# Attention and mixture of experts in one kernel: logits once per chunk, the first output product and half of the key work later, and p v in two halves

## The chip, the cores and the metric

The kernel runs on one core of a Trainium2 chip. The metric is the device time of one execution in microseconds, the median of several runs. TensorE (PE in the profile) does the matrix products into PSUM, VectorE (DVE) and ScalarE (ACT) move results from PSUM to SBUF and do the arithmetic between, GpSimd (POOL) works in SBUF, and SyncE (SP) issues most of the transfers.

## The reference

Four batches of 12288 queries of width 128 attend to 768 keys each, which are averages of 4 x 4 pixels through one weight matrix; keys and values are the same array. The attention's output is the input of a mixture of 8 experts, of which each token uses one.

```python
kv_pool = kv.reshape(B, H // r, r, W // r, r, C).mean(axis=(2, 4))
k = v = kv_pool.reshape(B, -1, C) @ w_sr
s = (q @ k.transpose(0, 2, 1)) / sqrt(C)
a = exp(s - s.max(-1)); a /= a.sum(-1) + 1e-09
x = a @ v                                   # 49152 tokens of 128
logits = x @ w_gate
e_idx = argmax(logits); gate_w = softmax(logits)[e_idx]
eom = 1 / (1 + exp(-(x @ w_output_gate)))
for e in range(E):                          # 8 experts
    h = maximum(x[mask] @ w1[e], 0)         # 128 -> 1024
    out[mask] = gate_w * eom[:, e] * (h @ w2[e])
```

## The kernel before

**Groups, chunks, rounds.** The tokens are worked in 96 groups of 512 (GT), 24 per batch; four groups are a chunk of 2048, for which the experts are chosen together (the last chunk is split into units of three groups and one). The main loop runs over rounds i, each of eight slots s. In round i the scores of group i are computed (slots 0, 2, 4 and 6, 128 tokens each), the product p v of group i-1, and the expert's two layers of an earlier group, with the expert that most tokens of the batch are taken to want, chosen from the mean of the keys. The tokens whose own choice is another expert are written to lists by GpSimd, 16 indirect transfers a chunk (L688), and worked at the end.

**Precision.** Each product of full precision is made of three products of half precision: a value is split into a high half (ScalarE, a copy with rounding) and a low half (VectorE, the difference), and high x high, high x low and low x high are added in PSUM. So a group's p v is 18 matmuls of 512 columns (6 key blocks x 3; L523), a product h of the first expert layer is 3 (L773 to L775), a product y of the second layer is 3 (L788 to L790), and 128 tokens' scores are 6 of 384 columns (L466 to L470).

**Order by hand.** The schedule is manual: every engine works in the order in which the loop issues. Within a slot the letters of `ORD = "shxryfue"` say what follows: s the scores (`qk`), h one product of the first layer (`moe_h`), x the exponential (`qk_exp`, ScalarE L487), r its rounding to two halves (ScalarE L500, GpSimd L501), y one product of the second layer (`moe_y`), u p v (`pv`, slot 5), e the events that were put off to this slot. The products y with f = 5, 6 and 7 come at the start of a slot, the others at y, where four h are ahead of them (`yb == hb - 4`). One slot in 30 leaves h and y out, so that they drift back against the scores.

**PSUM.** psA has two buffers of two banks for the scores. psH has three banks in turn under the tag "H": for every h, for U (the result of p v), for the logits `lg`, and for their transposes `lT`. psY has a single bank for Y, in which the eight products y of a group add up; ScalarE copies it to `ys` (L793) after f = 7, and the next group's f = 0 writes the bank anew. A product h is evicted by ScalarE (HH, L778) and then by VectorE (HL, L779); U by ScalarE (L527) and VectorE (L528) to U2.

**Logits.** `logits(i)` is called for each group, in slot 1 of round i+2. It multiplies U2's two halves by the gate weights, 32 columns wide (wgA and wgB), as 8 matmuls of 128 columns in four column strips of the array (L540, L543), and ScalarE copies the 128 columns of the result (L546). After a chunk's last group the four results are transposed (`logits_turn`, L564) and `routing` runs over the next slots, in steps on VectorE.

**Keys of the next batch.** `kv_prep` is a generator that does a step a slot: it pools the pixels on GpSimd, transposes and multiplies on TensorE (L301, L236), scales, and splits the keys to K2 (L342 on ScalarE, L343 on VectorE, in two halves of 384). V2 is a transposing transfer of K2. Then the mean of the keys times the gate weights chooses the expert (`choice`, L247, put as a hook into the scores of slot 0 or 2), `w_load` fetches its weights and `w_split` splits them (L754 to L761).

Of the kernel before, what the change touches and what calls it, by code (L numbers as in the profile page):

```python
# [20 lines left out]
F32 = mybir.dt.float32  # L21
# [4 lines left out]
AF = mybir.ActivationFunctionType  # L26
ALU = mybir.AluOpType
# [3 lines left out]
ts = bass.ts  # L31

P = 128
C = 128
E = 8
FF = 1024
NFB = FF // P
NK = 768
NKB = NK // P
GT = 512  # L40
GB = GT // P
# [5 lines left out]
PSH = 11  # L47
EPS = 1e-9
BIG = float(1 << 22)
LAG = 2  # L50
OL = 7
US2 = 2.0 ** -28


class Cfg:
# [27 lines left out]
    QL, QT, QN = 0, 3, 6  # L83
# [4 lines left out]
    QK = 2  # L88
    UT, UO = 3, 7
    UD, UDS = 0, 0  # L90
    UB = 9
    MT, MO = 4, 2
    KV0, KVP, KVD = (2, 1), (23, 23), 8
    PHD = (0, 2)
# [3 lines left out]
def body(ctx, tc, q, kv, w_sr, w_gate, w_og, w1, w2, out, cfg=Cfg):  # L98
    nc = tc.nc
    pe, act, dve, pool, sp = nc.tensor, nc.scalar, nc.vector, nc.gpsimd, nc.sync  # L100
    NB, NCH = cfg.NB, cfg.NC
    NG = NB * NCH * CG
# [3 lines left out]
    UN = [(c * CG, CG) for c in range(NCK - 1)]  # L106
# [3 lines left out]
    unit = {g0 + g: (u, g) for u, (g0, n) in enumerate(UN) for g in range(n)}  # L110
# [4 lines left out]
    rt = ctx.enter_context(tc.tile_pool(name="rt", bufs=1))  # L115
    psA = ctx.enter_context(tc.tile_pool(name="psA", bufs=2, space=PSUM))
    psH = ctx.enter_context(tc.tile_pool(name="psH", bufs=3, space=PSUM))
# [58 lines left out]
    wgA = cst.tile([P, 4 * E], F16, name="wgA")  # L176
    wgB = cst.tile([P, 4 * E], F16, name="wgB")
    g3 = cst.tile([P, 4], F32, name="g3")
# [13 lines left out]
    qscale = float(C) ** -0.5  # L192
# [35 lines left out]
    def kv_prep(b, fast):  # L228
# [17 lines left out]
        def choice(ap):  # L246
            pe.matmul(ap, sb, wg[:, 0:E], start=True, stop=True)  # L247
            got.append(ap)
# [22 lines left out]
        for k in range(NKB):  # L271
            while KVN[b][0] < 4 * (k + 1) or not fast and now[0] < KVI[(b, k)] + cfg.KVD:
                yield
            if fast:
                if k + 1 < NKB:
                    kv_add(b, k + 1)
                x, y = kvst.pop((b, k))
                ps = psA.tile([P, 2, 512], F32, tag="A", name=f"kvt{b}_{k}")
# [11 lines left out]
            x, y = kvst.pop((b, k))  # L290
# [9 lines left out]
            ps = psA.tile([P, 2, 512], F32, tag="A", name=f"kvt{b}_{k}")  # L300
# [8 lines left out]
        e2 = kvp.tile([P, 7], F32, tag="ve2", name=f"ve2{b}")  # L309
# [16 lines left out]
        ps = psA.tile([P, 2, 512], F32, tag="A", name=f"vmp{b}")  # L326
# [10 lines left out]
            chosen()  # L337
        K2 = kvp.tile([P, 2, NK], F16, tag="K2", name=f"K2{b}")
        V2 = kvp.tile([P, 2 * NKB, C], F16, tag="V2", name=f"V2{b}")
        for h in range(2):  # L340
            hh = ts(h, NK // 2)
            act.activation(K2[:, 0, hh], kT[:, hh], AF.Copy, scale=e2[:, 2:3])  # L342
            dve.scalar_tensor_tensor(K2[:, 1, hh], kT[:, hh], e2[:, 2:3], K2[:, 0, hh], op0=ALU.mult, op1=ALU.subtract)  # L343
            if not h:
                dve.tensor_scalar(e2[:, 3:4], e2[:, 0:1], 2.0 ** -14 * qscale, None, op0=ALU.mult)
                dve.tensor_scalar(e2[:, 4:5], e2[:, 2:3], US2, None, op0=ALU.mult)
                dve.tensor_scalar(e2[:, 5:6], e2[:, 4:5], EPS * 2.0 ** PSH, None, op0=ALU.mult)
        if fast:
            next(QP[0], None)
        KVT[b] = (K2, V2, e2[:, 3:4], e2[:, 4:6])  # L350
# [5 lines left out]
        if not fast:  # L356
            yield
            mean()
            hooks.append((now[0] + 1, lambda S: choice(S[:, 0, 384:384 + E])))
            while not got:  # L360
                yield
            yield
# [13 lines left out]
    KVT, CHO, CHI, WL, QP = {}, {}, {}, [], []  # L376


    QT, QM, QS, PTt, US, UF, UT, SUMS, LP, LG = {}, {}, {}, {}, {}, {}, {}, {}, {}, {}

    def tokens(ap3, i):

# [61 lines left out]
    hooks, now, mid = [], [0], [False]  # L444
# [73 lines left out]
    def pv(i, lo, hi, cols=slice(0, GT)):  # L518
        ops = pv_ops(i)
        if i not in PVP:  # L520
            PVP[i] = psH.tile([P, GT], F32, tag="H", name=f"U{i}")
        for n in range(lo, hi):
            pe.matmul(PVP[i][:, cols], ops[n][0], ops[n][1][:, cols], start=(n == 0), stop=(n == len(ops) - 1))  # L523
        if hi == len(ops) and cols.stop == GT:
            u = PVP.pop(i)
            U2 = wk.tile([P, 2, GT], F16, tag="U2", bufs=cfg.UB, name=f"U2{i}")
            act.activation(U2[:, 0, :], u, AF.Copy, scale=US2)  # L527
            dve.scalar_tensor_tensor(U2[:, 1, :], u, US2, U2[:, 0, :], op0=ALU.mult, op1=ALU.subtract)  # L528
            US[i] = (U2[:, 0, :], U2[:, 1, :])
            UF[i] = U2  # L530
            del PTt[i]

    def logits(i):

        UH, UL = US[i]
        c, g = unit[i]
        ps = psH.tile([P, GT], F32, tag="H", name=f"lg{i}")
        for j in range(GB):
            r = slice(32 * j, 32 * j + 32)
            pe.matmul(ps[r, 0:P], wgA, UH[:, ts(j, P)], start=True, stop=False, tile_position=(0, 32 * j))  # L540
        for j in range(GB):
            r = slice(32 * j, 32 * j + 32)
            pe.matmul(ps[r, 0:P], wgB, UL[:, ts(j, P)], start=False, stop=True, tile_position=(0, 32 * j))  # L543
        if g == 0:
            LP[c] = rt.tile([P, GT], F32, tag="lgp", bufs=1, name=f"lgp{c}")
        act.activation(LP[c][:, ts(g, P)], ps[:, 0:P], AF.Copy, scale=g3[:, 2:3])  # L546

    def u_turn(i):

# [232 lines left out]
    def moe_y(i, f):  # L782
        w2h, w2l = WT[i // GPB][2:4]
        HH, HL = HS.pop((i, f))
        if f == 0:
            YP[i] = psY.tile([P, GT], F32, tag="Y", name=f"Y{i}")
        Y = YP[i]
        pe.matmul(Y, w2h[:, ts(f, P)], HH, start=(f == 0), stop=False)  # L788
        pe.matmul(Y, w2l[:, ts(f, P)], HH, start=False, stop=False)  # L789
        pe.matmul(Y, w2h[:, ts(f, P)], HL, start=False, stop=(f == NFB - 1))  # L790
        if f == NFB - 1:
            ys = wk.tile([P, GT], F32, tag="ys", bufs=OL, name=f"ys{i}")
            act.activation(ys, YP.pop(i), AF.Copy)  # L793
            OST[i] = ys
            del US[i]
# [173 lines left out]
    with tc.manual_schedule(engines={pool.engine, sp.engine, pe.engine, act.engine, dve.engine}):  # L969
# [26 lines left out]
        hb = yb = 0  # L996
# [8 lines left out]
        def at(n, f, *args):  # L1005
            events.setdefault(8 * i + s + n, []).append((f, *args))

        def after_values(ri, rc):
            logits(ri)
            if rc is not None:  # L1010
                def turn():
                    logits_turn(rc)
                    rts.append([routing(rc), 0, rc])
                at(cfg.RG, turn)
            n = max(0, 8 * cfg.UD + cfg.UDS * ri - now[0])
            at(cfg.UT + n, u_turn, ri)
            at(cfg.UO + n, u_out, ri)
# [34 lines left out]
        for i in range(NG + OL):  # L1052
            att = i < NG
            pvi, ri, mi, oi = i - 1, i - 2, i - LAG, i - OL - 1
            if att and i % GPB == k0(i) and i // GPB + 1 < NB:
                kl, kp = kv_load(i // GPB + 1), kv_prep(i // GPB + 1, False)
            rc = unit[ri][0] if 0 <= ri < NG and ri + 1 == sum(UN[unit[ri][0]]) else None
            for s in range(8):
# [4 lines left out]
                if s == 0 and i in (NG - 1, NG):  # L1063
                    at(7, after_values, i - 1, unit[i - 1][0] if sum(UN[unit[i - 1][0]]) == i else None)
                go = mi >= 0 and not (att and (8 * i + s) % cfg.SK == cfg.SO)
                if go and yb % 8 >= 5 and yb < 8 * NG:
                    moe_y(*divmod(yb, 8))
                    yb += 1
                for o in cfg.ORD if mi >= 0 else cfg.ORDA:
                    if o == "h" and go:  # L1070
                        if hb < 8 * NG:
                            moe_h(*divmod(hb, 8))
                            hb += 1
                    if o == "s" and att and s % 2 == 0:
                        qk(i, s // 2)
                        while late:
                            qk_round(*late.pop(0))
                    if o == "x" and att and s % 2 == 0:
                        qk_exp(i, s // 2)
                    if o == "r" and att and s % 2:  # L1080
                        if s // 2 in cfg.PHD and i < LAG:
                            late.append((i, s // 2))
                        else:
                            qk_round(i, s // 2)
                    if o == "f" and s == cfg.PVS:
                        mid[0] = True
                        if ws:
                            next(ws, None)
                        mid[0] = False
                        if att and i % CG != 3:  # L1090
                            routes(1)
                    if o == "u":
                        for d, h in cfg.PVA:
                            x = i - d // 8
                            if d % 8 == s and 0 <= x < LAG - 1:
                                pv(x, 0, 3 * NKB, slice(h * GT // 2, (h + 1) * GT // 2))
                        if LAG - 1 <= pvi < NG and s == cfg.PVS:
                            pv(pvi, 0, 3 * NKB)
                    if o == "y" and go and yb == hb - 4:
                        moe_y(*divmod(yb, 8))  # L1100
                        yb += 1
                    if o == "e":
                        for f, *args in events.pop(8 * i + s, ()):
                            f(*args)
# [10 lines left out]
                if att and s in (cfg.QLA[i] if i < len(cfg.QLA) else (cfg.QL,)):  # L1115
# [5 lines left out]
                    while qa < qn:  # L1121
                        c = qa // CG
# [5 lines left out]
                if att and s == cfg.QL:  # L1128
                    n = min(ql + 2, i + cfg.QN + 1, NG)
# [7 lines left out]
                if kp:  # L1137
                    n = (8 * (i % GPB - k0(i)) + s) % cfg.KVP[min(i // GPB, 1)]
# [25 lines left out]
        while events:  # L1164
            i, s = divmod(min(events), 8)
# [39 lines left out]
```

## Time and profile before

| | |
|---|---|
| median of 3 runs | 1961.77 us (1961.56 to 1962.83) |
| the profiled execution | 1980.32 us, span 1978.6 us |
| TensorE busy | 1888.6 us, 95% of the span |
| VectorE, ScalarE, GpSimd busy | 1503.3, 1330.9, 1158.6 us |
| mean granted TensorE clock | 0.991 |
| queue of SyncE's transfers | 309.18 MB, 77.9% of 16 engines' time |

A matmul's record spans its whole passage through the array, so that consecutive ones overlap: a 512-column matmul lasts 0.38 us in the records, but the next one starts 0.215 us after it. The pace is read from the starts. "Idle before" is the time that an engine stood still in front of an instruction, and the arrow names what ended the wait.

### The profile page before, as it was taken

What the parts mean: (1) busy time and instruction counts of PE and PEld (TensorE: products, weight loads), DVE (VectorE), ACT (ScalarE), POOL (GpSimd) and SP (SyncE); (2) the same over time, 40 slices, a digit from 0 to 9 for tenths busy, and PEclk for the clock granted to TensorE, in tenths of its full rate; (3) what the DMA queues carried; (4) which work ended last, traced back from release to release, by engine and by line L of the source; (5) the groups of instructions that cost most, each with busy time, mean ns of one, the idle gap of its engine ahead of it and who ended that gap; (6) DMA issues with size and microseconds to landing.
All of it is one profiled execution on the core that took longest, in us unless ns stands there. A gap on an engine that the chain in (4) does not pass through costs nothing. (4 is left out here: it accounts for less than half of the span.)

```text
span 1978.6 us, 31039 instructions
## 1 busy us (share of the span) xinstructions
PE 1888.6 (95%) x10225; PEld 948.2 (48%) x10225; DVE 1503.3 (76%) x3005; ACT 1330.9 (67%) x2462; POOL 1158.6 (59%) x996
## 2 busy tenths in 40 slices
PE   6999999999999999999999999999999999999967
PEld 4444455444444544444444444444444444445434
DVE  6776777878878778778788787787787877886753
ACT  3767677667677776667776776666767767677623
POOL 3437567656576676663765756645556556456551
PEclk9999999999999999999999999999999999999999
DMA  7888888887888888787978888869688787877622
GB/s 234 156 164 162 171 160 179 159 163 154 165 174 166 182 165 160 158 167 153 166 167 167 171 170 177 159 135 181 135 159 159 140 166 156 143 158 140 130 63 67
DMA packets 884018, 311.64 MB, mean 158 GB/s; under 512 B 827584, under 2 KB 833857, under 8 KB 883856
## 3 DMA queue, kind: packets, MB, share of 16 engines
q1 hardware_dynamic: 870944, 309.18, 77.9%
q0 software_dynamic: 12480, 0.40, 0.5%
q8 instruction: 81, 1.33, 0.3%
q14 instruction: 81, 0.66, 0.1%
q10 hardware_dynamic: 432, 0.07, 0.0%
HBM read 56.83 MB, written 51.25 MB: 55 GB/s over the span
## 5 line engine op out<-in xcount | busy, mean ns | idle before, releaser
L501 POOL TENSOR_TENSOR ph<-pr,ph 128x768 f16<-128x768 f32 x384 | 632.3, 1647 | 651.4 <-ACT ph L500 383.6
L779 DVE SCALAR_TENSOR_TENSOR HL<-H,HH 128x512 f16<-128x512 f32 x768 | 526.9, 686 | 164.5 <-ACT HH L778 124.4
L778 ACT ACTIVATE HH<-H 128x512 f16<-128x512 f32 x768 | 455.1, 593 | 237.6 <-PE H L775 192.9
L487 ACT ACTIVATE pr<-S,nm,qm 128x768 f32<-128x768 f32 x384 | 380.5, 991 | 175.5 <-DVE nm L473 140.0
L688 POOL DMA_INDIRECT scr<-rw,idx x384 | 382.7, 997 | 95.0 <-issue 86.0
L472 DVE TENSOR_REDUCE nm<-S 128x1 f32<-128x768 f32 x384 | 365.0, 951 | 43.3 <-PE S L470 35.2
L523 PE MATMUL U<-PT,V 128*128 128x512 f16 (+1 forms) x1746 | 392.4, 379 | 5.8 <-DVE HL L779 3.4
L500 ACT ACTIVATE ph<-pr 128x768 f16<-128x768 f32 x380 | 319.7, 841 | 2.4 <-DMA PT<-ph 1.7
L773 PE MATMUL H<-U,w 128*128 128x512 f16 x768 | 292.0, 380 | 14.2 <-DVE HL L779 11.8
L788 PE MATMUL Y<-HH,w 128*128 128x512 f16 x768 | 291.7, 380 | 9.4 <-ACT ys L793 8.0
L790 PE MATMUL Y<-HL,w 128*128 128x512 f16 x768 | 291.3, 379 | 1.2 <-issue 1.0
L774 PE MATMUL H<-U,w 128*128 128x512 f16 x768 | 292.0, 380 | 0.0
L775 PE MATMUL H<-U,w 128*128 128x512 f16 x768 | 291.9, 380 | 0.0
L789 PE MATMUL Y<-HH,w 128*128 128x512 f16 x768 | 291.3, 379 | 0.2 <-issue 0.2
L523 PEld LDWEIGHTS <-V 128*128 128x128 f16 x1746 | 172.0, 99 | 211.3 <-issue 9.9
L466 PE MATMUL S<-K,qT 128*128 128x384 f16 x768 | 188.9, 328 | 15.3 <-ACT pr L487 6.4
L470 PE MATMUL S<-K,qT 128*128 128x384 f16 x768 | 188.5, 327 | 1.3 <-DVE qT L442 1.3
L468 PE MATMUL S<-K,qT 128*128 128x384 f16 x768 | 188.4, 327 | 0.5 <-DVE K L343 0.5
L527 ACT ACTIVATE U<-U 128x512 f16<-128x512 f32 x96 | 57.2, 596 | 136.1 <-PE U L523 129.6
L528 DVE SCALAR_TENSOR_TENSOR U<-U,U 128x512 f16<-128x512 f32 x96 | 66.1, 688 | 100.9 <-ACT U L527 77.0
L808 DVE TENSOR_TENSOR o<-S,msw 128x256 f32<-128x256 f32 x176 | 74.7, 425 | 85.9 <-ACT pr L487 75.0
L789 PEld LDWEIGHTS <-w 128*128 128x128 f16 x768 | 75.2, 98 | 97.3 <-issue 16.3
(209 smaller groups left out, 1924.0 us busy)
## 6 DMA issues: line engine op xcount, KB each, us to landing
kvs<-in_kv_dram SPq DMA_DIRECT2D x96, 256.0 KB
q<-in_q_dram SPq DMA_DIRECT2D x96, 256.0 KB
urows<-uT SPq DMA_DIRECT2D x96, 256.0 KB
out_dram<-o SPq DMA_DIRECT2D x96, 256.0 KB
PT<-ph SPq DMA_TRANSPOSE x384
scr<-rw,idx POOLq DMA_INDIRECT x384
wr<-in_moe_w_dram SPq DMA_DIRECT2D x8, 512.0 KB
tw<-in_moe_w_dram SPq DMA_DIRECT2D x4, 512.0 KB
```

Of the source, the lines that this page charges most:

```text
L472: dve.tensor_reduce(out=nm[:, 0:1], in_=S[:, :, 0:384], op=ALU.max, axis=AX.XY, negate=True)
L487: act.activation(pr.rearrange("p (a k) -> p a k", a=2), S[:, :, 0:384], AF.Exp, bias=nm[:, 1:2], scale=es, accum_out=SUMS[c][:, bl:bl + 1])
L500: act.activation(ph[:, 0, :], pr, AF.Copy)
L501: pool.tensor_tensor(ph[:, 1, :], pr, ph[:, 0, :], op=ALU.subtract)
L523: pe.matmul(PVP[i][:, cols], ops[n][0], ops[n][1][:, cols], start=(n == 0), stop=(n == len(ops) - 1))
L688: ins = pool.indirect_dma_start(out=scr, out_offset=bass.IndirectOffsetOnAxis(ap=idx[:, bl:bl + 1], axis=0), in_=rw[:, bl, :], in_offset=None,
L773: pe.matmul(H, w1h[:, ts(f, P)], UH, start=True, stop=False)
L774: pe.matmul(H, w1h[:, ts(f, P)], UL, start=False, stop=False)
L775: pe.matmul(H, w1l[:, ts(f, P)], UH, start=False, stop=True)
L778: act.activation(HH, H, AF.Relu)
L779: dve.scalar_tensor_tensor(HL, H, 0.0, HH, op0=ALU.max, op1=ALU.subtract)
L789: pe.matmul(Y, w2l[:, ts(f, P)], HH, start=False, stop=False)
```

## The change

There are four parts, and the number of buffers for U2 goes from 9 to 6 (`UB`).

1. `logits` is called once per unit (chunk), after its last group, and issues the matmuls of all its groups in a row into one bank, with one copy of up to 512 columns by ScalarE. `LU` holds the groups' U2 until then.
2. The product y with f = 0 waits until five h are ahead of it, and is then issued together with f = 1 (`YE = 1`). The branch with `YF` stays unused (0).
3. `kv_prep` outside the first batch issues the four operations on the keys' halves in four slots, high 0, high 1, low 0, low 1, in place of one. The hook for `choice` is due 4 slots after the mean in place of 1 (`CHD`).
4. The 18 matmuls of p v are issued nine in slot 5 and nine in slot 6 (`PVU`).

```diff
-    UB = 9
+    UB = 6
+    YF, YE = 0, 1
+    CHD = 4
+    PVU = ((5, 0, 9), (6, 9, 18))
...
+        high_key(halves[0])
+        if fast:
+            low_key(halves[0])
...
+        if not fast:
+            yield
+        high_key(halves[1])
+        if not fast:
+            yield
+            low_key(halves[0])
+            yield
+        low_key(halves[1])
...
-            hooks.append((now[0] + 1, lambda S: choice(S[:, 0, 384:384 + E])))
+            hooks.append((now[0] + cfg.CHD, lambda S: choice(S[:, 0, 384:384 + E])))
...
-            US[i] = (U2[:, 0, :], U2[:, 1, :])
+            LU[i] = US[i] = (U2[:, 0, :], U2[:, 1, :])
...
+    def logits(c):
+
+        g0, ng = UN[c]
+        ps = psH.tile([P, GT], F32, tag="H", name=f"lg{c}")
+        for g in range(ng):
+            for n, w in enumerate((wgA, wgB)):
+                for j in range(GB):
+                    r = slice(32 * j, 32 * j + 32)
+                    pe.matmul(ps[r, ts(g, P)], w, LU[g0 + g][n][:, ts(j, P)], start=(n == 0), stop=(n == 1),
+                              tile_position=(0, 32 * j))
+        for g in range(ng):
+            del LU[g0 + g]
+        LP[c] = rt.tile([P, GT], F32, tag="lgp", bufs=1, name=f"lgp{c}")
+        act.activation(LP[c][:, 0:ng * P], ps[:, 0:ng * P], AF.Copy, scale=g3[:, 2:3])
...
         def after_values(ri, rc):
-            logits(ri)
             if rc is not None:
+                logits(rc)
+
...
-                        if LAG - 1 <= pvi < NG and s == cfg.PVS:
-                            pv(pvi, 0, 3 * NKB)
-                    if o == "y" and go and yb == hb - 4:
-                        moe_y(*divmod(yb, 8))
-                        yb += 1
+                        for x, lo, hi in cfg.PVU:
+                            if LAG - 1 <= pvi < NG and s == x:
+                                pv(pvi, lo, hi)
+                    if o == "y" and go and yb == hb - 4 - (cfg.YE and hb < 8 * NG and yb % 8 == 0):
+                        for _ in range(1 + (yb == hb - 5)):
+                            moe_y(*divmod(yb, 8))
+                            yb += 1
```

## Rows read from the trace of the kernel before

**Rows 1.** The page, part 1: busy us, share of the span, instructions.

```profile
PE 1888.6 (95%) x10225; PEld 948.2 (48%) x10225; DVE 1503.3 (76%) x3005; ACT 1330.9 (67%) x2462; POOL 1158.6 (59%) x996
```

**Rows 2.** Stretches: length, busy us (instructions) by engine; granted clock, DMA share, GB/s.

```profile
core 0: us, PE busy (x) PEld busy (x) DVE busy (x) ACT busy (x) POOL busy (x), PEclk, DMA share, GB/s
60.00:1880.00 1820.00, 1776.92 (x9619) 882.50 (x9618) 1417.69 (x2757) 1273.98 (x2353) 1104.96 (x932) 1.00 0.82 161
1200.00:1400.00 200.00, 189.28 (x1009) 93.06 (x1008) 157.94 (x317) 134.60 (x250) 112.81 (x95) 0.98 0.80 159
1600.00:1800.00 200.00, 199.35 (x1082) 99.17 (x1080) 157.81 (x314) 140.70 (x258) 111.08 (x93) 1.00 0.80 153
```

**Rows 3.** Waits of TensorE: us in total, times, longest us.

```profile
PE H L773 <- DVE HL L779: 11.8, 22, 1.8
PE Y L788 <- ACT ys L793: 8.0, 11, 2.1
PE U L523 <- DVE HL L779: 3.4, 4, 1.4
PE lg L540 <- DVE HL L779: 2.1, 5, 0.6
PE H L773 <- ACT lgp L546: 1.6, 2, 1.0
```

**Rows 4.** Waits of ScalarE: the remote ones.

```profile
ACT HH L778 <- remote: 18.3, 3, 8.0
```

**Rows 5.** Timeline of TensorE around one group's logits: start us, us, instruction.

```profile
1011.61 0.38 PE L789 MATMUL Y<-HH,w 128*128 128x512 f16 x1
1011.83 0.38 PE L790 MATMUL Y<-HL,w 128*128 128x512 f16 x1
1012.13 0.24 PE L540 MATMUL lg<-U,wgA 128*32 128x128 f16 x4
1012.20 0.23 PE L543 MATMUL lg<-U,wgB 128*32 128x128 f16 x4
1012.36 0.50 PE L466 MATMUL S<-K,qT 128*128 128x384 f16 x2
...
1013.35 0.38 PE L773 MATMUL H<-U,w 128*128 128x512 f16 x1
```

**Rows 6.** Groups of instructions by form: xcount, busy us, mean ns, idle before.

```profile
L543 PEld LDWEIGHTS <-wgB 128*32 128x32 f16 x384 | 10.1, 95 | 0.0
...
L793 ACT ACTIVATE ys<-Y 128x512 f32<-128x512 f32 x96 | 56.7, 591 | 1.3 <-PE Y L790 0.7
L546 ACT ACTIVATE lgp<-lg,g 128x128 f32<-128x128 f32 x96 | 35.0, 364 | 0.2 <-PE lg L543 0.2
```

**Rows 7.** Timeline of TensorE: three of its eleven waits for ys.

```profile
525.38 0.38 PE L788 MATMUL Y<-HH,w 128*128 128x512 f16 x1 [1.58 <-ACT ys L793]
...
1010.10 0.38 PE L788 MATMUL Y<-HH,w 128*128 128x512 f16 x1 [0.75 <-ACT ys L793]
...
1396.07 0.38 PE L788 MATMUL Y<-HH,w 128*128 128x512 f16 x1 [2.08 <-ACT ys L793]
```

**Rows 8.** Timeline where the keys of batch 1 are split.

```profile
406.02 0.62 DVE L343 SCALAR_TENSOR_TENSOR K<-kT,ve,K 128x384 f16<-128x384 f32 x1 [0.68 <-ACT K L342]
...
406.87 0.61 DVE L343 SCALAR_TENSOR_TENSOR K<-kT,ve,K 128x384 f16<-128x384 f32 x1
...
409.25 0.38 PE L773 MATMUL H<-U,w 128*128 128x512 f16 x1 [1.84 <-DVE HL L779]
```

**Rows 9.** Last work on batch 1's weights; stretch with all of batch 0's L773.

```profile
L761 POOL TENSOR_TENSOR w<-wr,w x4: 1167/1172/1173, 489.8 to 508.6; 128x512 f16<-128x512 f32 x4
...
0.00:535.00 535.00, 73.25 (x192) 18.89 (x192) 0.99 0.83 170
```

**Rows 10.** Timeline around the p v of one group and its eviction.

```profile
1019.99 4.05 PE L523 MATMUL U<-PT,V 128*128 128x512 f16 x18
1023.88 0.38 PE L788 MATMUL Y<-HH,w 128*128 128x512 f16 x1
...
1024.08 0.60 ACT L527 ACTIVATE U<-U 128x512 f16<-128x512 f32 x1 [2.21 <-PE U L523]
...
1024.70 0.69 DVE L528 SCALAR_TENSOR_TENSOR U<-U,U 128x512 f16<-128x512 f32 x1 [0.90 <-ACT U L527]
```

**Rows 11.** Waits of ScalarE for a product h.

```profile
ACT HH L778 <- PE H L775: 192.9, 201, 4.2
```

**Rows 12.** Groups of ScalarE: the exponential and the read of its sum.

```profile
L487 ACT ACTIVATE pr<-S,nm,qm 128x768 f32<-128x768 f32 x384 | 380.5, 991 | 175.5 <-DVE nm L473 140.0
...
L487 ACT ACTIVATION_READ_ACCUMULATOR pr<-S,nm,qm 128x1 f32 x384 | 73.8, 192 | 0.0
```

More of the change, by code (lines that the diff above doesn't have):

```diff
@@ L339, in kv_prep, with high_key, low_key @@
         V2 = kvp.tile([P, 2 * NKB, C], F16, tag="V2", name=f"V2{b}")
-        for h in range(2):
-            hh = ts(h, NK // 2)
+        halves = [ts(h, NK // 2) for h in range(2)]
+        def high_key(hh):
             act.activation(K2[:, 0, hh], kT[:, hh], AF.Copy, scale=e2[:, 2:3])
+        def low_key(hh):
             dve.scalar_tensor_tensor(K2[:, 1, hh], kT[:, hh], e2[:, 2:3], K2[:, 0, hh], op0=ALU.mult, op1=ALU.subtract)
[L344 to L347, printed above, removed]
+        high_key(halves[0])
+        if fast:
+            low_key(halves[0])
+        dve.tensor_scalar(e2[:, 3:4], e2[:, 0:1], 2.0 ** -14 * qscale, None, op0=ALU.mult)
+        dve.tensor_scalar(e2[:, 4:5], e2[:, 2:3], US2, None, op0=ALU.mult)
+        dve.tensor_scalar(e2[:, 5:6], e2[:, 4:5], EPS * 2.0 ** PSH, None, op0=ALU.mult)
+        if not fast:
[6 more added lines that the diff above has]
+        low_key(halves[1])
         if fast:
@@ L376, in body @@
     KVT, CHO, CHI, WL, QP = {}, {}, {}, [], []
-    QT, QM, QS, PTt, US, UF, UT, SUMS, LP, LG = {}, {}, {}, {}, {}, {}, {}, {}, {}, {}
+    QT, QM, QS, PTt, US, LU, UF, UT, SUMS, LP, LG = {}, {}, {}, {}, {}, {}, {}, {}, {}, {}, {}
     def tokens(ap3, i):
@@ L528, in pv @@
             dve.scalar_tensor_tensor(U2[:, 1, :], u, US2, U2[:, 0, :], op0=ALU.mult, op1=ALU.subtract)
-            US[i] = (U2[:, 0, :], U2[:, 1, :])
+            LU[i] = US[i] = (U2[:, 0, :], U2[:, 1, :])
             UF[i] = U2
             del PTt[i]
[L533 to L546, printed above, removed]
+    def logits(c):
[11 more added lines that the diff above has]
+        act.activation(LP[c][:, 0:ng * P], ps[:, 0:ng * P], AF.Copy, scale=g3[:, 2:3])
     def u_turn(i):
@@ L1065, in body @@
                 go = mi >= 0 and not (att and (8 * i + s) % cfg.SK == cfg.SO)
-                if go and yb % 8 >= 5 and yb < 8 * NG:
-                    moe_y(*divmod(yb, 8))
-                    yb += 1
+                for _ in range(1 + (cfg.YF and yb % 8 == 6)):
+                    if go and yb % 8 >= 5 and yb < 8 * NG:
+                        moe_y(*divmod(yb, 8))
+                        yb += 1
                 for o in cfg.ORD if mi >= 0 else cfg.ORDA:
@@ L1096, in body @@
                                 pv(x, 0, 3 * NKB, slice(h * GT // 2, (h + 1) * GT // 2))
-                        if LAG - 1 <= pvi < NG and s == cfg.PVS:
-                            pv(pvi, 0, 3 * NKB)
-                    if o == "y" and go and yb == hb - 4:
-                        moe_y(*divmod(yb, 8))
-                        yb += 1
+                        for x, lo, hi in cfg.PVU:
[3 more added lines that the diff above has]
+                        for _ in range(1 + (yb == hb - 5)):
+                            moe_y(*divmod(yb, 8))
+                            yb += 1
                     if o == "e":
```

## The prediction

> **What bounds the kernel now.** I read the busy line of the page first, then stretches of the span, then TensorE's waits, and last the order of instructions around the lines that the change touches. TensorE is busy for 1888.6 of 1978.6 us [rows 1]. In the steady part, from 60 to 1880 us, it is idle for 1820 - 1776.9 = 43 us [rows 2]. From 1200 to 1400 us it lacks 10.7 us, from 1600 to 1800 only 0.65: the keys of a next batch are prepared in the first of these stretches and not in the second. So there are two ways to make this kernel faster: fewer TensorE cycles, or those 43 us. VectorE (1417.7 us in the same 1820) and ScalarE (1274.0) are not full on average, but they lag for a few us at a time, and that is what TensorE's waits show [rows 3]. The waits that the change can reach are those for a free buffer of psH (11.8 us before L773, 3.4 before L523, 2.1 before L540, 1.6 for the copy of the logits) and for the evicted Y (8.0 before L788): 26.9 us, of which 1.1 lies after 1880.
>
> The profiled execution took 1980.32 us, 1.7 more than its span; the median of the runs is 1961.77. The 18.55 us between them are nearly the 18.3 us that ScalarE waited three times for something remote [rows 4], all of them after 1886 us. I take this as a part of the profiled execution that the change leaves alone, and subtract the same gain from both.
>
> **Logits in one burst.** Now every group issues 8 matmuls into four column strips. The last full matmul before them starts at 1011.83 and the next full one at 1012.36 [rows 5]; a full matmul is followed after 0.215 (1011.61 to 1011.83, the one in front), so the 8 cost 0.53 - 0.215 = 0.315 us. The second four start 0.07 after the first, so two sets are 0.14 and about 0.18 are bubbles at the two ends, where the weights of the strips are not loaded ahead. A burst of 8 sets is then 0.18 + 8 x 0.07 = 0.74, against 4 x 0.315 = 1.26: 0.52 saved in 23 chunks and 0.34 in the unit of three groups, 12.3 us. If each set has to wait for its own weight load, 0.095 [rows 6], the burst is 0.94 and the saving 7.5 us; if the bubbles return with every group, it is nothing. Ends 0 and -12.3; I take -11, nearest to the measured pitch of the sets. The row shows the four matmuls of a set within 0.24 us, hardly longer than the 0.23 of one, so they start within about 0.01. The Trainium skill speaks against a gain of this size (TensorE: Matmul & The Clock Gate, "Wait — 56ns, not 53.3ns?"): starts of matmuls never come closer than about 25 ns. By that rule 32 of them would take 0.8 us and bubbles on top, an estimate of some 0.3 saved per chunk, 7 us in all; this trace's four starts within 0.01 us disagree for matmuls on different strips, and the sum goes by the row.
>
> ScalarE copies 24 times about 0.59 (like the 128x512 copy of L793) in place of 96 times 0.364 [rows 6]: 35.0 - 14.2 = 21 us less work, worth nothing by itself, but it and the psH buffer that three of four groups no longer take relieve the waits below.
>
> **First output product later.** The wait for Y's eviction falls in slots where the product f=0 follows f=7 of the group before too closely. It now comes a slot later, so at least one h, three matmuls or 0.65 us, lies between. Eleven waits sum to 8.0; two are long (1.58 and 2.08) and keep 0.9 and 1.4, the others are at most 0.75 [rows 7]. I count -5.4; ends 0 and -8.0. The six matmuls of the double slot are the same work; five HH and HL buffers hold the five that are now outstanding, and the sixth is written after the first has been read.
>
> **Lower halves of the keys later.** In one slot VectorE gets two L343 of 0.61 in front of the max of the scores and HL, and TensorE then waits 1.84 us for HL [rows 8]. With the four operations in four slots, 1.2 of it should go. The same place comes in each of three preparations (with a 1.20 and a 1.20 plus 0.34): -4.3 in all, a part of the 11.8; ends 0 and -4.9. What is late next: the keys are ready 3 slots later, and the matmul that chooses the expert is put off to the next slot 0 or 2 that the hooks allow, which I count as a whole round (20 us) later. The weights of batch 1 were split by 508.6 + 1.2, and 192 products h, those of batch 0, are issued only by 535 us [rows 9]. A cover of 25 us becomes 5. Without it TensorE would stand at the first h of the batch, some us once; I count 0.
>
> **Products p v in two rows of nine.** The 18 matmuls take 3.9 us, from 1019.99 to 1023.88 [rows 10], in which TensorE gives ScalarE and VectorE nothing to evict; ScalarE idles 192.9 us for H alone [rows 11] and is short elsewhere in the round. Halved, the pause comes twice and the backlog drains sooner. So I let half of the other psH waits go: (11.8 - 1.1 - 4.9) + 3.4 + 2.1 + 1.6 = 12.9, half -6.5; ends 0 and -12.9.
>
> The price: U's buffer is held into the next slot. psH has three buffers in turn, so the h two after the last p v needs U's. Between them stood a slot with scores more; now it is one h, one y and one set of scores, 6 x 0.215 + 0.99 = 2.3 us (scores: 1012.36 to 1013.35, rows 5). The eviction of U ends 1024.70 + 0.69, so 1.5 us after the last p v is issued [rows 10]. The slack falls to 0.8 us, 0.1 where that slot has no y. Behind a waiting h stand all later products on TensorE. Ends: 0, and +38 if U is delayed by one exponential in every one of 92 rounds (0.99 + 0.19 [rows 12], less 0.8: 0.41 each); I take +4, as ScalarE mostly stands idle before U now. The last two groups evict U in 1.5 us under 1.3 us of products: +0.4.
>
> U2 has 6 buffers in place of 9. The sixth-last group's h are done a round or more before the buffer is written, and the chunk's logits half a round before: 0.
>
> **Clock.** From 1200 to 1400 us the granted clock averages 0.98 [rows 2]: some 4 us lost, next to the waits. Fewer waits should bring some back, -1.5; ends 0 and -4.
>
> **Sum.** -11 - 5.4 - 4.3 - 6.5 + 4 + 0.4 - 1.5 = -24.3. On the profiled execution: 1980.3 - 24 = 1956. On the median: 1961.8 - 24 = **1938 us**, likely 1929 to 1948.
>
> **Rivals.** *All of it comes*: the burst at its measured pitch (-12.3), all reachable waits of the steady part (-25.8), the clock's 4 us, no price: -42, 1920. For it: 1600 to 1800 us shows TensorE full for 200 us. Against: waits on VectorE for counts and scores stay, and a backlog shows elsewhere. *The waits only move*: ScalarE and VectorE are late for reasons that stay (routing, the keys' chain), and a wait removed at h comes back at the scores; only the burst counts: 1951. For it: the waits gather where extra VectorE work lies. Against: both engines have over 20% free. *U's buffer* (the other side): the h of slot 0 waits for U's eviction behind an exponential in every round, +38 in place of +4: 1938 + 34 = 1972, slower. It decides from 0.3 us per round. For it: slack 0.8, and 0.1 in some rounds. Against: in the trace U starts 0.2 us after the last p v is issued over. *It does nothing*: the bubbles return with every group, and U's price eats the waits: 1962.
>
> **Chances.** Forecast 0.58, all of it 0.12, waits move 0.14, U's buffer 0.09, nothing 0.07. About 0.2% (3.9 us) is what a measurement of this kernel can tell from no change. Faster: 0.58 + 0.12 + 0.13 = 0.83; same: 0.07 and the edges of the third and fourth, 0.09; slower 0.08. The range 1924 to 1960 leaves out most of "all of it", "U's buffer" and half of "nothing".
>
> **What would show it.** L540 and L543 24 times in a row of 32 with under 0.8 us between the full matmuls around them; the wait of L788 for L793 below 3 us; no wait of over 1 us at h just after the keys' halves; L523 in pairs of nine, and ScalarE's idle time for L775 shorter. Wrong, if L773 waits for L528, which it never does now, for more than 10 us; if the burst takes over 1 us; or if TensorE's idle time in the steady part stays at 40 us.

## The result and the profile after

The changed kernel takes 1943.58 us (median, 1941.83 to 1944.66), the kernel before 1962.22 in the same set of runs: 0.9904 of it, 95% interval 0.9887 to 0.9921, 18.6 us less. The forecast was 1938 in 1924 to 1960. The time is inside, also inside the narrower range of the forecast's own case (1929 to 1948); but one term of the sum was too small and the others together much too large, and that is what the rest is about.

The kernel before took 1960 to 1962 us in some sets of runs and 1976 to 1979 in others. The difference lies behind the main part: in a repeat of the changed kernel in a set of the second kind ScalarE waited 15.2 us for something remote, from 1865 us on, as in [rows 4], and in the profile of its first set not at all. So below, kernels of different sets are compared by their ratio to the kernel before in their own set, and by the length of the main part: from the first matmul of group 0's p v to the first of group 95's. That is 1842.5 us before (43.06 to 1885.59), 1823.5 after (43.71 to 1867.22) and 1824.0 in the repeat.

The page of the changed kernel, part 1, and two stretches (columns as in rows 2), first of the kernel before and then of the changed one:

```profile
PE 1870.8 (96%) x10225; PEld 951.0 (49%) x10225; DVE 1504.7 (77%) x3005; ACT 1321.3 (68%) x2391; POOL 1159.8 (60%) x996
```

```profile
43.06:1885.59 1842.53, 1796.74 (x9724) 893.62 (x9725) 1433.75 (x2791) 1288.51 (x2377) 1118.77 (x943) 1.00 0.82 160
60.00:1850.00 1790.00, 1746.92 (x9453) 867.44 (x9452) 1396.43 (x2716) 1254.57 (x2318) 1085.29 (x914) 1.00 0.82 161
```

```profile
43.71:1867.22 1823.51, 1781.48 (x9723) 897.70 (x9724) 1436.06 (x2792) 1279.55 (x2307) 1120.96 (x944) 0.99 0.82 162
60.00:1850.00 1790.00, 1750.89 (x9542) 880.47 (x9540) 1413.37 (x2744) 1256.31 (x2268) 1097.15 (x925) 1.00 0.82 163
```

In the main part TensorE's busy time fell by 15.3 us (1796.74 to 1781.48) and its idle time by 3.8. In 60 to 1850 us it is idle for 39.1 us, where the kernel before has 43.1; the repeat has 41.6. So the gain is mostly work that TensorE no longer has, and little of it waits. The burst, in the timeline of TensorE:

```profile
1042.82 0.38 PE L807 MATMUL Y<-HL,w 128*128 128x512 f16 x1
1043.13 0.24 PE L558 MATMUL lg<-U,wgA 128*32 128x128 f16 x4
1043.19 0.23 PE L558 MATMUL lg<-U,wgB 128*32 128x128 f16 x4
1043.25 0.23 PE L558 MATMUL lg<-U,wgA 128*32 128x128 f16 x4
...
1043.53 0.23 PE L558 MATMUL lg<-U,wgB 128*32 128x128 f16 x4
1043.69 0.50 PE L483 MATMUL S<-K,qT 128*128 128x384 f16 x2
```

From the last full matmul to the next one 0.87 us, less 0.215: 0.655 us for 32 matmuls, against 4 x 0.315 before [rows 5]. That is 0.605 saved in 23 chunks and 0.4 in the unit of three groups: 14.3 us. Eight sets start within 0.40 us, on average 0.057 apart.

TensorE's waits (us in total, times, longest), to be held against [rows 3], and under them three lines of the kernel before that are not in those rows:

```profile
PE S L483 <- ACT pr L504: 7.5, 6, 1.7
PE H L790 <- DVE HL L796: 7.0, 12, 1.3
PE S L822 <- ACT pr L504: 6.6, 5, 2.5
...
PE U L540 <- DVE HL L796: 5.1, 6, 1.7
PE H L790 <- DVE U L545: 4.7, 11, 1.0
PE S L642 <- DVE oh L637: 3.6, 1, 3.6
...
PE lT L581 <- ACT lgp L563: 1.6, 3, 0.5
...
PE Y L805 <- ACT ys L810: 0.3, 1, 0.3
```

```profile
PE S L466 <- ACT pr L487: 6.4, 6, 1.5
PE S L805 <- issue: 4.0, 4, 2.4
...
PE S L625 <- DVE oh L620: 1.6, 1, 1.6
```

Of the waits that the parts aimed at, these fell: h for HL from 11.8 to 7.0, the first output product from 8.0 to 0.3, the logits' own wait (2.1) and h's for the logits' copy (1.6) to nothing, 16.2 us in all. The forecast's three terms (5.4, 4.3 and 6.5) add up to the same figure, but that is chance: the first product gave 7.7 where 5.4 was counted, the waits for psH 8.5 where 10.8 was. And 14.5 came back in other places: h for U's eviction 4.7 (new), the transposes lT for the larger copy 1.6 (new), p v for HL 3.4 to 5.1, the counts for their sums 1.6 to 3.6, and the waits of scores and transposes for psA, where L822's grew from 4.0 to 7.4 (with two small ones not shown) and L483's for the exponential from 6.4 to 7.5. In the repeat the transposes wait 4.6 us, so this balance moves by some 3 us between two executions.

### The profile page after: what moved, and what is told of

It is laid out like the page before. It is cut to its first block, busy times and chain, and to the rows that moved or that the text cites. A ratio compares the mean times of both kernels' runs of the same rounds, so it can differ in the third digit from the quotient of the medians.

```text
span 1942.9 us, 31028 instructions
## 1 busy us (share of the span) xinstructions
PE 1870.8 (96%) x10225; PEld 951.0 (49%) x10225; DVE 1504.7 (77%) x3005; ACT 1321.3 (68%) x2391; POOL 1159.8 (60%) x996
## 5 line engine op out<-in xcount | busy, mean ns | idle before, releaser
L795 ACT ACTIVATE HH<-H 128x512 f16<-128x512 f32 x768 | 456.5, 594 | 246.6 <-PE H L792 240.3
L540 PE MATMUL U<-PT,V 128*128 128x512 f16 (+1 forms) x1746 | 406.1, 378 | 7.4 <-DVE HL L796 5.1
L790 PE MATMUL H<-U,w 128*128 128x512 f16 x768 | 292.3, 381 | 12.3 <-DVE HL L796 7.0
L483 PE MATMUL S<-K,qT 128*128 128x384 f16 x768 | 189.2, 328 | 13.1 <-ACT pr L504 7.5
L792 PEld LDWEIGHTS <-w 128*128 128x128 f16 x768 | 75.3, 98 | 91.4 <-issue 1.4
L807 PEld LDWEIGHTS <-w 128*128 128x128 f16 x768 | 75.2, 98 | 90.8 <-issue 0.3
L805 PEld LDWEIGHTS <-w 128*128 128x128 f16 x768 | 75.2, 98 | 88.3 <-issue 0.5
```

The lines of the kernel that those rows point to most:

```text
L790: pe.matmul(H, w1h[:, ts(f, P)], UH, start=True, stop=False)
L792: pe.matmul(H, w1l[:, ts(f, P)], UH, start=False, stop=True)
L795: act.activation(HH, H, AF.Relu)
```

## The experiments

Every ratio below is to the kernel before in the same set of runs, with its 95% interval. The kernels made from the one before keep nine buffers for U2, those made from the changed one have six; the number of buffers was not run by itself.

**The burst undone** (`logits` called per group as before, the other three parts kept).

```diff
...
         def after_values(ri, rc):
+            logits(ri)
             if rc is not None:
-                logits(rc)
-
...
```

> The changed kernel with the logits of each group by themselves again (8 matmuls in slot 1 of every round, 96 copies of 128 columns); the other three parts stay. Theory A (the burst is the gain, the waits that the other parts remove come back elsewhere): in the changed kernel a burst of 32 takes 0.655 us between full matmuls against 4 x 0.315, so undoing it costs 0.6 x 23 + 0.4 = 14 us: 1957 to 1959. Theory B (my forecast: each part is worth its own term): undoing it costs 11 to 12, and the psH waits that the burst relieves come back, some 4 more: the same 1958, with over 8 us of waits of L773's successor for HL. Theory C (the parts depend on each other: two rows of p v only work with fewer logits tiles in psH): over 1963, slower than the kernel before.

Measured: 1958.21 us, 0.9985 of before (0.9976 to 0.9994). Without the burst the three other parts gain 2.9 us; undoing it cost 14 to 16 us by the ratios (0.9914 and 0.9904 with it, in two sets). Theory C falls. Theories A and B had named the same time, but B had also named more waits of h for HL, and they are there, twice as long as with the burst (7.0):

```profile
PE H L790 <- DVE HL L796: 15.4, 25, 2.2
```

**The burst alone** (the kernel before with part 1).

> The kernel before with the burst of logits alone. Theory A: 1962.2 - 14.3 = 1948, plus or minus 2, with TensorE's idle time in the steady part still near 43 us. Theory B: 1951, plus the relief of psH, some 4: 1947. Theory C, that the burst by itself does all: 1943 to 1945, like the changed kernel, so the other three parts are worth nothing.

Measured: 1947.49, 0.9933 (0.992 to 0.9947): 13 us, near the 14.3 of the trace. Its main part is 16.1 us shorter than before, and its idle time is still 45.4 us:

```profile
60.00:1850.00 1790.00, 1744.64 (x9520) 877.44 (x9521) 1407.13 (x2739) 1254.10 (x2263) 1095.83 (x922) 1.00 0.82 162
```

```profile
PE Y L788 <- ACT ys L793: 14.8, 18, 2.1
...
PE H L773 <- DVE HL L779: 3.5, 6, 1.1
```

This bears out theory A. The burst by itself takes h's wait for HL from 11.8 to 3.5 us, and the first output product then waits 14.8 for ys in place of 8.0: the wait moved. Theory C of that expectation is less likely: the changed kernel is at 0.9904 and 0.9914 in two sets, so the other parts add some 4 to 6 us, but the second interval (0.9901 to 0.9927) overlaps with that of the burst alone.

**The first output product in its old slot** (`YE = 0`).

> The changed kernel with the first output product in its old slot (YE = 0). Theory A: the wait of the first product for ys comes back in the records (some 8 us), but other waits shrink by as much: within 2 us of 1943.6. Theory B: the term of the forecast, +5.4: 1949.

Measured: 1944.53, 0.9919 (0.9905 to 0.9933). The wait of the first product for ys is 11.3 us in its records, and the kernel is, by its ratio, 1 to 3 us slower than the changed one (0.9904 and 0.9914 in two sets), with intervals that overlap. Its main part is no longer (1822.9 us, against 1823.5 and 1824.0):

```profile
PE Y L805 <- ACT ys L810: 11.3, 15, 2.1
...
PE H L790 <- DVE HL L796: 5.2, 7, 1.7
PE S L822 <- ACT pr L504: 5.1, 5, 2.5
PE U L540 <- DVE HL L796: 3.8, 4, 1.9
...
PE H L790 <- DVE U L545: 2.5, 8, 0.3
```

In the same kernel h waits 4.0 us less for HL and U, and p v for HL and the transposes for the exponential 2.8 less, as they would if the engines behind these waits caught up while TensorE stands for ys.

**p v in one row** (`PVU = ((5, 0, 18),)`).

> The changed kernel with the 18 matmuls of p v in slot 5 again. Theory A: within 2 us of 1943.6; the new wait of h for U's eviction (4.7 us) goes and the others grow. Theory B: +2.5 (half of the psH waits back, -4 for the price of the held buffer): 1946. Rival C: the split is a loss, as 4.7 us of new waits stand against a fall of HL waits that the burst alone brings: 1939 to 1941, faster than the changed kernel.

Measured: 1948.79, 0.9936 (0.9922 to 0.9949), 4 to 6 us slower than the changed kernel by the ratios. Rival C falls: beside all the other parts the two rows help, by more than I had counted.

**A control, and the keys in one slot** (the four operations in one slot again, `CHD = 1`).

> The changed kernel unaltered, as the control beside the others of this set: 0.9904 of the kernel before, as measured first (0.9887 to 0.9921).

> The changed kernel with the four operations on the keys' halves in one slot again and the choice's hook one slot after the mean. Burst alone gave 0.9933, burst with late first product and late keys 0.9936 (p v undone), so by theory A' (late keys and late first product are worth nothing, the two rows of nine bring what the burst leaves) this is within 2 us of the control. By my forecast's term it is 4.3 us slower, with waits of h for HL of 1.2 to 1.8 us back just after each preparation of keys.

Measured: the control 0.9914 (0.9901 to 0.9927), the keys in one slot 0.993 (0.9918 to 0.9943). 3 us apart by ratio and 4.3 by the medians, with intervals that overlap: the forecast's 4.3 is not refuted, and theory A' is not either. With the keys in one slot h waits 9.8 us for HL, against 6.5 in the control. But its waits just after the keys' halves are 0.96 us after the first preparation, nothing after the second and 0.64 after the third, not the 1.2 to 1.8 expected; the changed kernel has one of 1.01 after its third. In the changed kernel VectorE's two operations are 2.2 us apart, and from 405 to 425 us TensorE waits for nothing, where it waited 1.84 us for HL [rows 8]:

```profile
411.21 0.61 DVE L349 SCALAR_TENSOR_TENSOR K<-kT,ve,K 128x384 f16<-128x384 f32 x1
413.45 0.61 DVE L349 SCALAR_TENSOR_TENSOR K<-kT,ve,K 128x384 f16<-128x384 f32 x1
```

**The burst and the two rows, without the other two parts.**

```diff
+    PVU = ((5, 0, 9), (6, 9, 18))
...
-                        if LAG - 1 <= pvi < NG and s == cfg.PVS:
-                            pv(pvi, 0, 3 * NKB)
+                        for x, lo, hi in cfg.PVU:
+                            if LAG - 1 <= pvi < NG and s == x:
+                                pv(pvi, lo, hi)
...
```

The edit of the burst, which is in this kernel too, is that of part 1.

> The kernel before with the burst and the two rows of nine, without the other two parts. Theory A': the same as the control within 2 us, 0.990 of the kernel before, though the wait of the first product for ys is in its records (8 to 15 us). Theory B (each part its own term): 5.4 + 4.3 slower than the control, 0.995. Theory C (two rows are worth something only where the first product is late): 0.993, like the burst alone.

Measured: 0.9962 (0.9949 to 0.9975), 9.5 us slower than the control of the set (0.9914). By its distance from the control that is theory B's time: 5.4 and 4.3 are 9.7. But its reason, that each part is worth a term of its own, does not hold, as four kernels with the burst show:

| with the burst | product and keys in their old slots | product and keys late |
|---|---|---|
| p v in one row | 0.9933 | 0.9936 |
| p v in two rows | 0.9962 | 0.9904 and 0.9914 |

The late product and the late keys are worth nothing beside one row, and 9.5 us beside two in the same set. The two rows cost 5.7 us in the first column and gain 4 to 6 in the second. TensorE's waits of the kernel with the burst and the two rows:

```profile
PE Y L789 <- ACT ys L794: 9.8, 14, 2.1
PE H L774 <- DVE HL L780: 7.8, 12, 1.2
...
PE lT L565 <- ACT lgp L547: 4.8, 6, 1.3
...
PE H L774 <- DVE U L529: 3.0, 7, 1.0
```

**The two rows alone** (the same edit in the kernel before).

> The kernel before with the two rows of nine alone. On top of the burst alone (0.9933) the two rows made the kernel slower (0.9962), with the first chunk's wait for the routing's sums at 3.6 us in place of 1.6. Theory D (the split by itself costs: U's buffer is held longer and a round has no pause in which VectorE and ScalarE catch up; only the other parts make room for it): slower than before, by up to 7 us, 1.000 to 1.004, with waits of L773 for U in the records. My forecast's term: 6.5 gained less 4 for the held buffer, 2.5 faster, 0.9987. Rival: the split helps by itself and the loss in the pair comes from the burst's copy of 512 columns: 0.995 or less.

Measured: 1964.03, 1.0014 of before (1.0005 to 1.0023), 2.7 us slower by the ratio. The time is theory D's, and the waits for U are there; h waits longer for HL, not shorter (15.1 us against 11.8).

```profile
PE H L774 <- DVE HL L780: 15.1, 19, 2.0
...
PE S L626 <- DVE oh L621: 3.6, 1, 3.6
PE H L774 <- DVE U L529: 3.0, 7, 1.0
```

But other waits shrank, that for ys from 8.0 to 5.0, and the idle time in 60 to 1850 us is 43.0 us, as before (43.1):

```profile
60.00:1850.00 1790.00, 1747.04 (x9441) 866.73 (x9440) 1403.95 (x2713) 1255.87 (x2315) 1085.99 (x913) 1.00 0.82 161
```

So the loss is not more waiting in all. It is as large as what TensorE's clock took: the eleven runs list a mean granted clock (the share of TensorE's full rate) of 0.9935 on average, those of the kernel before in the set 0.9949, and 0.0014 of 1962 us is 2.7, an estimate.

By the same estimate, each kernel against the one before in its own set, the clock took some 3 us of the 5.7 that the two rows cost beside the burst (0.9904 against 0.9925, with 0.9944 against 0.9951 for the burst alone), and some 3 of the 4 to 6 that they gain beside all parts (0.9928 against 0.9951 for the single row, with 0.9918 against 0.9925 for the control). The estimate takes all time at the lower clock as lost in proportion. The clock differs between runs of one kernel too: the five with p v in a single row go from 1945.72 us at 0.995 to 1951.83 at 0.991. How much of it comes from a kernel's waits and how much from chance is not shown.

**The counts' hook a slot later in the first eight rounds.** In each kernel with two rows and the old hook TensorE waits 3.6 us at 127 us: the matmul of the first chunk's counts (L642) is ahead of the scores of slot 6 in TensorE's order, and its sums are not ready. Timeline of the changed kernel, and a stretch of it:

```profile
127.34 0.19 PE L642 MATMUL S<-oh,ones 128*128 128x8 f16 x1 [3.57 <-DVE oh L637]
...
129.29 0.63 PE L790 MATMUL H<-U,w 128*128 128x512 f16 x1
129.71 0.63 PE L791 MATMUL H<-U,w 128*128 128x512 f16 x1
```

```profile
120.00:135.00 15.00, 11.43 (x44) 4.68 (x43) 10.99 (x24) 5.89 (x12) 3.28 (x2) 0.77 0.83 147
```

Behind the wait the matmuls start 0.42 us apart, not 0.215: the array runs at its lower level, 1.2 GHz, and the granted clock of the 15 us is 0.77, which is 3.4 us lost in all (where the kernel before has 1.00). A wait of 2.51 us at 775 is followed by it as well, but not in every profile: the kernel with the later hook, below, has the same wait at 774 and keeps its clock. First the changed kernel, then that one:

```profile
770.00:785.00 15.00, 12.15 (x56) 6.05 (x54) 9.19 (x16) 10.47 (x21) 10.89 (x10) 0.89 0.91 185
```

```profile
770.00:785.00 15.00, 12.15 (x63) 6.09 (x62) 9.05 (x16) 11.02 (x23) 11.17 (x10) 1.00 0.97 192
```

```diff
-            hooks.append((now[0] + 1, counts))
+            hooks.append((now[0] + 1 + (now[0] < 8 * (OL + 1)), counts))
```

> The changed kernel with one more edit: in the first eight rounds the hook for the counts of the routing is due a slot later. In the changed kernel TensorE waits 3.57 us for the sums of the first chunk at 127 us, and its clock is at half for some 3.4 us behind it, so 3.57 + 1.7 = 5 us are there. If the wait goes without another in its place: 3 to 5 us faster than the control, 1939 to 1941 on the first scale; if the backlog of VectorE only shows at the scores: within 1 us.

Measured: 1956.01 where the control of the set has 1959.01 and before 1976.02: 0.9897 (0.9883 to 0.9911). The long wait and the lower clock are gone (the same stretch of this kernel, 120 to 135 us):

```profile
120.00:135.00 15.00, 13.90 (x72) 6.61 (x70) 13.42 (x29) 8.68 (x18) 3.63 (x3) 1.00 0.92 160
```

The six rounds from group 2's p v to group 8's take 112.67 us in place of 115.18 in the control. This is the fastest version found, 20 us below the kernel before; against the changed kernel it is 3 us by the medians of the set, with intervals that overlap.

**The two rows in slots 4 and 5** (with the later hook).

```diff
-    PVU = ((5, 0, 9), (6, 9, 18))
+    PVU = ((4, 0, 9), (5, 9, 18))
```

> The kernel with the later hook for the counts (0.9897 of before) and the two rows of nine in slots 4 and 5 in place of 5 and 6. If the wait of h for U's eviction comes from the buffer that is held up to the h two further on, it goes, as a slot with scores now lies between: 4.7 us of waits away, some 3 us faster, 0.988. If the transposed probabilities of the last 128 tokens land too late for slot 4, L540 waits for the transfer in many rounds: slower, over 0.992, with waits of L540 for PT in the records.

Measured: 0.9923 (0.991 to 0.9937), some 5 us slower by the ratios than with slots 5 and 6 (0.9897), with intervals that just overlap. Its waits:

```profile
PE S L483 <- ACT pr L504: 8.2, 6, 2.8
...
PE U L540 <- DMA PT<-ph: 3.5, 4, 2.3
...
PE H L790 <- DVE U L545: 1.0, 1, 1.0
```

The place of the price was right: U's wait is 1.0 in place of 4.7. The time is that of the other side, but not for its reason: the transfer is waited for 3.5 us, against 2.4 in the changed kernel. The scores wait longer for the exponential, but most of the loss is again the clock: in the profiles the main part is 4.7 us longer than with slots 5 and 6, and it loses 10.2 us to the lower clock, against 3.4.

**The transposes of the logits a slot later** (with the later hook).

```diff
-    RG = 1
+    RG = 2
```

> The kernel with the later hook for the counts (0.9897 of before) and the logits' transposes two slots after the burst in place of one. The transposes wait for ScalarE's copy of 512 columns in 6 of 24 chunks, 4.4 us in all. If these are net losses: 3 to 4 us faster, 0.988. If TensorE's pause there only gives VectorE and ScalarE time that they need anyway: within 1 us, 0.990.

Measured: 1982.97, 1.0115 (1.0097 to 1.0132), over 20 us slower than before: a clear miss. The hook also starts the routing, whose steps are taken in even slots, so all its VectorE work came two slots later in the round. Idle time in 60 to 1850 us is 69.5 us, with these waits:

```profile
PE H L790 <- DVE HL L796: 17.3, 21, 2.1
PE U L540 <- DVE HL L796: 10.9, 17, 1.4
...
PE Y L807 <- DVE HL L796: 7.0, 7, 1.5
```

**The burst a slot earlier, the routing where it was** (with the later hook).

```diff
-    RM = 1
+    RM = 0
...
-    RG = 1
+    RG = 2
...
-    UT, UO = 3, 7
+    UT, UO = 4, 8
```

> The kernel with the later hook for the counts (0.9897 of before), the burst of logits a slot earlier (slot 0), the transposes in the slot where they are now, so that the routing keeps its slots (the transfers of U2 keep theirs too). Moving the whole routing made the kernel 2% slower; this moves only what stands ahead of it. Theory E (the routing's slots on VectorE decide, the logits' place does not): 0.988 to 0.990, the waits of the transposes for ScalarE's copy (4.4 us) gone. Rival (waits move): a wait of the burst for the last group's U2, or of an h for a psH buffer, takes their place: 0.990 to 0.993.

Measured: 0.991 (0.9896 to 0.9923), in the rival's range and no gain on the later hook alone (0.9897). The waits of the transposes fell from 4.4 to 1.3 us, and h's for HL grew from 8.1 to 12.4. The run before had lost 39.6 us in the main part against the kernel with the later hook; with the transposes and the routing in their slots it is 4.1. So that run lost by the later slots of the transposes and the routing, and two slots between the burst and the transposes do little. Which step of the routing it is, is not shown.

## Why the prediction was right, and where it was not

**What bounds the kernel**: right. TensorE is 96% busy after as well, and the one part that takes work from it gives 13 of the 18.6 us.

**The burst**: right in kind, too small. -11 was taken between 0 and -12.3; it is -14.3 in the trace and -13 timed. The pitch of a set, 0.07, was read from a single step between sets, the first behind an entry; over the eight sets of a burst it is 0.057. By the Trainium skill's least distance of starts (TensorE: Matmul & The Clock Gate, "Wait — 56ns, not 53.3ns?"), about 25 ns, 32 matmuls would take 0.8 us, an estimate. The trace has their starts within some 0.4 us, 14 ns each on average. For matmuls on strips of their own columns that distance does not hold here, and the measurement decides.

**First output product and keys**: the waits went, and the step "what of it lies on the path" failed. I took a wait of TensorE that goes as time gained, and each part as a term of its own. The changed kernel's idle time stayed at 39 to 42 us, the one of the prediction's three signs of being wrong that came. 14.5 of 16.2 us of waits came back elsewhere, and two kernels show the exchange: without the late product, 11.3 us for ys stand against 6.8 less in four other waits; with the burst alone, h waits 8.3 less for HL and the first product 6.8 more for ys. The two parts together were counted at 9.7. Beside the two rows they are worth 9.5, which repays what the two rows cost; beside a single row they are worth nothing. Undone one by one they cost 1 to 3 and 3 to 4 us, within the noise.

**Half of the other psH waits**: put down to the wrong part. The two rows should have halved them, but alone they raise h's wait for HL from 11.8 to 15.1 us, and the three parts without the burst have 15.4. It is the burst that takes this wait away (3.5 us), a relief that the prediction mentions and gives no term of its own. ScalarE's idle time for L775, which should have become shorter, is 240.3 us in place of 192.9 [rows 11], and 213.0 with p v in a single row.

**The two rows of nine**: the term of -6.5 + 4 does not exist as one number. Alone they cost 2.7 us, on the burst 5.7, and with the late product and the late keys beside them they gain 4 to 6; by the estimate above about 3 us of each is the clock, and the gain of 1 to 3 that is left without it is inside the noise. U's price was well placed (4.7 us of waits, and 1.0 with the rows in slots 4 and 5) and near its size; the wait for the first chunk's sums, 2 us longer in every kernel with two rows but those with a later hook, I had not looked for. By which wait the two rows depend on the other two parts is not shown.

**The sum**: the parts other than the burst were counted at 13.3 us, and 5.6 of the 18.6 are left for them beside the burst's 13. In total waiting the second rival, "the waits only move", to which I gave 0.14, comes nearer than the forecast; its time, 1951, does not. That the forecast's time came within 6 us is in part luck: a burst 2 to 3 us larger than counted covered a part of what the others fell short by.

**The clock**: no gain. From 60 us on, the main part loses 3.4 us to it before, and 6.8 and 3.4 in two profiles after; a longer single wait (3.57) now stands at the beginning.

**What was counted at nothing**: the choice of the expert came a round later (441 in place of 422 us), and the weights of batch 1 were done at 525.9 + 1.2 us, 5 us ahead of the first h that uses them, the 193rd, at 532.2. The cover was as thin as said (5 us) and held:

```profile
L778 POOL TENSOR_TENSOR w<-wr,w x4: 1152/1160/1172, 504.8 to 525.9; 128x512 f16<-128x512 f32 x4
```

**The remote waits**: that the change leaves them alone is right, that they belong to the profiled execution is not: they belong to a set of runs.

What is open: in the rounds in which keys are prepared two runs of the same kernel differ by up to 1.5 us in six rounds (115.01 and 116.49 us from the eighth on), so terms below 3 us can't be separated by these runs. Whether six buffers for U2 in place of nine cost anything is open as well.

## What to carry to other kernels

Where one engine is 95% busy, count first what its instructions cost and what comes off. A wait that goes is not yet time gained: here 14.5 of 16.2 us came back in other waits, so ask which engine used the pause to catch up. Work that switches the array to column strips belongs together: here each entry and exit cost about 0.2 us, and a set of four strips 0.057. In a schedule written by hand, test a part beside the others that it will run with: here one part changed its sign. And compare the granted clocks of the runs before a difference of a few us is put down to an edit.

## What the runs showed of the hardware

A single wait of TensorE of 3.57 us was followed by some us at 1.2 GHz (starts 0.42 us apart) in each profile that has it, and cost 5 to 7 us with it (1.7 and 3.4 us of clock in two profiles of the changed kernel). Waits of 2.51 us were followed by it in some profiles and not in others (granted clock 0.89 and 1.00 around the same wait). Runs of one kernel differ by it: 1945.72 us at a mean granted clock of 0.995, 1951.83 at 0.991. Four matmuls on four column strips start within 0.02 us, and the load of the next strips' weights (0.095 us) does not hold up a set every 0.057 us.
